# Two output banks taken in turn, and the free one lent to ScalarE, in an attention kernel planned by its own scheduler

## The chip, the cores and the metric

The kernel runs on one core of a Trainium2 chip. Its time is the device time of one execution in microseconds (us), as the median of several runs. Five engines work side by side, each through its own list of instructions in order: TensorE (PE, matmuls; PEld is its weight load), VectorE (DVE), ScalarE (ACT), GpSimd (POOL) and SyncE (SP, which here issues the transfers). They wait for each other by semaphores. Matmuls write to PSUM, which has eight banks of 512 fp32 columns on each of 128 partitions.

## The reference

Attention with normalised queries and keys over 32 heads, 2048 positions and 20 elements a head, bfloat16 in and out:

```python
B, H, S, D = 1, 32, 2048, 640        # Dh = D // H = 20
qn = q / (jnp.sqrt((q * q).sum(axis=-1, keepdims=True)) + eps)
kn = k / (jnp.sqrt((k * k).sum(axis=-1, keepdims=True)) + eps)
logits = jnp.einsum('bhqd,bhkd->bhqk', qn, kn) * t[None, :, None, None]
attn = _softmax(logits, axis=-1)
return jnp.einsum('bhqk,bhkd->bhqd', attn, v)
```

The logits lie between -t and t, so no maximum is subtracted: the kernel sums exp(logit) times v, with a column of ones beside v for the denominator, and divides at the end.

## The kernel before

**Tiling.** The scores of a head are 2048 keys by 2048 queries. They are held as S^T: 128 keys on the partitions by 512 queries in one PSUM bank is a *unit*, of which a head has 64. A product with 20 elements uses 32 of TensorE's 128 rows, so up to four units' QK matmuls (row groups g) run at the same time. Four units, one of each g, make a group; the PV product of a group is four matmuls side by side in the four column groups of TensorE, which add into the four 32-partition strips of one bank, psO (`pv_mm`, L1089). All PV products of a head add into psO; then DVE transposes the bank into SBUF (`tr`, L1107), two small DVE operations divide, and SP stores.

**Two ways to the exponential.** The 16 groups of a head are shared out by DVE_TILES (L715): so many groups (5 to 8) of the head are *DVE tiles*, the rest belongs to ScalarE (*A units*, four to a group).
- A units: TensorE writes a *wave* of units into psA (five banks), and one ScalarE instruction (L1165) turns the whole wave into bfloat16 in `p_ring`, a ring of 40 slots, one unit each. Waves have 2 and 3 units by turns (WAVES, L694): even waves use banks 0 and 1 of psA (slot 0), odd waves banks 2 to 4 (slot 1). A wave's QK (`q3A`, L1073) waits for the exponential of the wave before the last, which read the same banks. Every group of four units becomes one PV group (`pvA`).
- DVE tiles: two matmuls (`q2D`, L1078) write psD (two banks). DVE reads them with an operation that makes the bit pattern of the exponential (`t1`, L1216, into `xt`), and three more phases of the same pattern are made from `xt` by integer additions: by POOL (L1246, `ss`), or by DVE (L1234, `sp`, or L1236, `ss`). A tile has four PV groups, one of each phase.

psA 5 banks, psD 2 and psO 1 are all eight banks of PSUM.

**Heads.** As there is one output bank, the first PV group of a head waits for the transpose of the head before (`pv_base`, L1100). TensorE may do QK in the meantime. Loads, norms, and the rotated copies of the keys (`kR`) for the heads ahead are made by SP and DVE beside this.

**The planner.** Nothing of the order is fixed by hand. Every instruction is a `Task` with an engine, a planned duration, dependencies and a priority (a due time counted in heads). `list_schedule` (L151) plays through the execution with these durations and writes down an order for each engine; `plan_waits` puts in the semaphore waits and `emit` the instructions. The planned duration of a matmul group is PE_MM (L712), and a change between QK and PV costs TensorE 0.097 us (L581 and L413). The choices between ready tasks depend on some twenty settings (KNOBS, L103), which change every 10 us of planned time to the values packed into STAGES (L108). When TensorE has nothing to do, the plan may put in a filler (`pvnil`, L1004), a PV group with zero weights. The waves are laid out before the planning (L787) as tasks like all others.

Of the kernel before, what the change touches and what calls it, by code (L numbers as in the profile page):

```python
# [54 lines left out]
class Task:  # L55
    __slots__ = ("eng", "fn", "dur", "deps", "pri", "name", "lat", "dma", "n", "users",
                 "start", "end", "seq", "inc", "cnt", "rows", "work", "modes", "win", "trig",
                 "alt", "parts", "parent", "rem", "glue", "room", "next", "head", "wide", "slow", "sdur", "pair", "base", "two", "need")

    def __init__(self, eng, name, fn, dur, deps, pri, lat=0.0, dma=None):  # L60
        self.eng, self.name, self.fn, self.dur = eng, name, fn, dur
        self.deps = [d for d in deps if d is not None]
        self.pri, self.lat, self.dma = pri, lat, dma
        self.inc, self.cnt = False, 0
        self.rows, self.work, self.modes = 128, 512.0, None
        self.win, self.trig = 0.0, None
        self.alt, self.parts, self.parent, self.rem = None, [], None, 0
        self.glue, self.room, self.next, self.head, self.wide = [], 0.0, None, None, None


        self.slow, self.sdur, self.pair, self.base, self.two = False, 0.0, None, dur, None

        self.need = None
# [5 lines left out]
class Program:  # L79
# [27 lines left out]
        "WAITH": (0.3, 0.1, 0.6), "BLOG": (5, 3, 4, 7, 9, 99), "PTWO": (1, 0), "STAY": (1, 0), "URGE": (3, 2, 4, 6), "BOOST": (1.0, 0.0, 0.4, 4.0), "DPV": (0.0, 0.3, 0.65, 1.0)}  # L107
    STAGES = (121198495550, 386731570679, 77123854022, 617480453033, 541694991365, 26516008980, 28188130953, 628587374903, 9557073731, 415555843896, 209498320437, 646470623202, 136583393724, 671941958076, 672324246996, 792421957682, 689380213680, 803027612629, 379997812126, 638643698950, 639121345246, 531136220444, 376259042864, 376617779119, 221897598895, 374543095684, 221362179218, 787313552789, 415913386058, 208446558798, 427204335065, 465723747116, 401404110210, 428458674786, 432937268058, 619977817991, 207993392811, 516782334303, 568560126277, 529856924852, 435260979089, 428752721390, 619855720106, 632747624100, 787539313032, 787849807561, 633115376521, 774950211778, 788266765840, 736861074358, 722791283681, 515990522269, 287562967953, 747408491084, 537279315194, 325670581757, 376196432267)  # L108

    def __init__(self):  # L110
        self.tasks = []
        self.nsw = 0
        self.filler, self.fillers = None, []

# [5 lines left out]
    def schedule(self):  # L120
        self.list_schedule()
        for f in self.tasks:
            if f.parts:
                for u in f.users:
                    u.deps = [d for d in u.deps if d is not f] + f.parts
        self.tasks = list(dict.fromkeys(t for f in self.tasks for t in f.parts or [f])) + self.fillers
# [24 lines left out]
    def list_schedule(self, until=None):  # L151
        self.stage = None
        for t in self.tasks:
# [4 lines left out]
            if t.alt:  # L158
                t.eng, t.parts, t.slow, t.dur = "DVE", [], False, t.base
        for i, t in enumerate(self.tasks):  # L160
            t.seq = i
            deps = []
            for d in t.deps:
                deps += d() if callable(d) else [d]
            t.deps = list(dict.fromkeys(deps))
            t.n = len(t.deps)
            for d in t.deps:
                d.users.append(t)
# [16 lines left out]
        def hold(e, now, dur):  # L185

            return any(now < w <= now + (self.HTR if self.tasks[q].name[:2] == "tr" else self.HOLD[e]) and now + dur > w + 0.03
                       for q, w in soon[e].items())

# [18 lines left out]

        def leave(t, now):

            for u in t.users:
                lat = t.lat if t.dma else (
                    self.SEM_LAT[t.eng] if u.eng != t.eng or t.eng == "POOL" else 0.12 if t.eng == "DVE" else 0.0)
                if u.eng == "PE" and u.name[:2] == "pv":
                    lat += self.TR_SLACK if t.name[:2] == "tr" else self.PV_SLACK
                rt[u.seq] = max(rt[u.seq], t.end + lat)
# [176 lines left out]
        left = collections.Counter(t.head for t in self.tasks if t.head is not None)  # L393
# [3 lines left out]
        def fill(now):  # L397
# [10 lines left out]
            t = self.filler()  # L408
# [3 lines left out]
            if last_pe[0] != "pv":  # L412
                t.end += max(0.0, 0.097 - (now - free["PE"]))  # L413
# [8 lines left out]
        while events or ready["POOL"]:  # L422
# [13 lines left out]
            while events and events[0][0] <= now:  # L436
                _, kind, _, t = heapq.heappop(events)
                touched.add(t.eng)
                if kind == 0:
# [3 lines left out]
            for e in touched:  # L443
# [7 lines left out]
                if e in soon:  # L451
                    wide = e == "PE" and self.QHOLD and any(
                        now < w <= now + self.QHOLD and self.tasks[q].name[2] == "A" for q, w in soon["PE"].items())
# [8 lines left out]
                if e == "PE":  # L462
# [4 lines left out]
                    else:  # L467
                        x = min(ready[e], key=lambda r: (r[0] + (0.0 if r[2].name[:2] == last_pe[0] else self.SWITCH) + (self.DPV if r[2].need and r[2].need[0] == "t" else 0.0) - (
                            self.BOOST if r[2].need and at_[r[2].need[0]] + self.URGE >= r[2].need[1] else 0.0), r[1]))
# [8 lines left out]
                elif e == "DVE" and self.CONT:  # L478
# [21 lines left out]
                    elif not sh:  # L500
                        x = min(ready[e])
                    else:
# [5 lines left out]
                        continue  # L508
                    ready[e].remove(x)
# [68 lines left out]
                if e == "PE":  # L578
                    kind = "pv" if t.rows > 128 else t.name[:2]
                    if kind != last_pe[0]:  # L580
                        t.end += max(0.0, 0.097 - (now - free["PE"]))  # L581
# [10 lines left out]
                if t.name[:3] in ("exp", "t1."):  # L592
                    at_[t.name[0]] += 1
                done += 1
                heapq.heappush(events, (t.end, 1, t.seq, t))
                if e == "DVE" and t.parent is None and t.users and t.users[0].alt and t.users[0].parts == [t]:
# [26 lines left out]
        assert until is not None or done == len(self.tasks), "dependence cycle"  # L623
# [58 lines left out]
def bass_standalone__qk_norm__prompt_kernel(  # L682
# [11 lines left out]
    WAVES = (2, 3)  # L694
    GORD = (0, 2, 1, 3)
# [16 lines left out]
    PE_MM = 0.223  # L712
    MORE = 12
    DLM = 2
    DVE_TILES = [5, 6, 6, 6, 7, 6, 7, 6, 7, 6, 7, 6, 7, 6, 7, 6, 6, 7, 6, 7, 6, 7, 6, 7, 6, 7, 6, 7, 6, 6, 7, 8]  # L715
# [9 lines left out]
    with ExitStack() as es:  # L725
# [33 lines left out]
        psA = es.enter_context(nc.psum_tensor("psA", [128, sum(WAVES) * 512], F32))  # L759
        psD = es.enter_context(nc.psum_tensor("psD", [128, 1024], F32))  # L760
        psO = es.enter_context(nc.psum_tensor("psO", [128, 512], F32))
# [25 lines left out]
        waves = []  # L787
        while not waves or waves[-1][-1] < NA - 1:
            i = waves[-1][-1] + 1 if waves else 0
            waves.append(list(range(i, min(i + WAVES[len(waves) % 2], NA))))  # L790
        wave_of = {u: w for w, us in enumerate(waves) for u in us}
# [207 lines left out]
        for i in range(NWARM):  # L999
            warm.append(add("PE", "warm", lambda e, tk: e.matmul(psO[:, :], ones[:, 0:128], ones[:, :], start=True, stop=True), PE_MM,  # L1000
# [3 lines left out]
        def null_mm(eng):  # L1004
            last = None
            for g in range(NG):
                last = eng.matmul(psO[32 * g:32 * g + 32, :], nil[:, :], ones[:, :], start=False, stop=False,  # L1007
                                  skip_group_check=True, tile_position=(0, 32 * g))
            return last
        prog.filler = lambda: Task("PE", "pvnil", lambda e, tk: null_mm(e), PE_MM, [z_nil, z_one], 0.0)  # L1010

        def first_head(rinv):
# [25 lines left out]
            tq = add("PE", "tq0", lambda e, tk: (tmm(e, psD[:, 512:1024], qsrc, 0, 2), tmm(e, psA[:, 1536:2048], qsrc, 2, 4))[1], 0.35, [nq, z_id], -200)  # L1038
            tk1 = add("PE", "tk0", lambda e, tk: tmm(e, psA[:, 2048:2560], kx[:, 0:512], 0, 2), 0.15, [nk1, z_id], -201)
            tk_ = add("PE", "tk0", lambda e, tk: tmm(e, psD[:, 0:512], kx[:, 0:512], 2, 4), 0.2, [nk, z_id], -199)  # L1040
            for i in range(NWARM2):
                warm.append(add("PE", "warm", lambda e, tk: e.matmul(psO[:, :], ones[:, 0:128], ones[:, :], start=True, stop=True), PE_MM, [tk_], -198))
            ka = add("ACT", "cpka", lambda e, tk: e.activation(
                qkT[0][:, 512:768], psA[:, 2048:2304], ACT.Copy), 0.33, [tk1], -90.5)
            q0.append(add("ACT", "cpq0", lambda e, tk: e.activation(qkT[0][:, 0:256], psD[:, 512:768], ACT.Copy), 0.33, [tq], -90))
            q0.append(add("DVE", "cpq0", lambda e, tk: e.tensor_copy(qkT[0][:, 256:512], psA[:, 1792:2048]), 0.34, [tq], -26.5))
# [42 lines left out]
        def pv_mm(eng, h, w_of, rhs_of):  # L1089
# [3 lines left out]
            for g in range(NG):  # L1093
                last = eng.matmul(psO[32 * g:32 * g + 32, :], w_of(g), rhs_of(g), start=start,  # L1094
# [5 lines left out]
        def pv_base(h):  # L1100
            return [ld_v[h]] + z_v[h % NV] + ([lambda: [trO[h - 1]]] if h else warm)

        def add_fin(h):
# [4 lines left out]
                oT_all[:, so, :, :].rearrange("p r d -> p (r d)"), psO[:, :]), 0.63,  # L1108
# [33 lines left out]
        def add_wave(w):  # L1142
            us = waves[w]
            slot = w % 2
            hs = sorted({A_units[i][0] for i in us})
            def f_qk(eng):
                last = None
                for i in range(len(us)):
                    h, r, g = A_units[us[i]]
                    last = qk_mm(eng, h, r, g, psA[:, (slot * WAVES[0] + i) * 512:(slot * WAVES[0] + i + 1) * 512])  # L1150
                return last
            deps = [act.get(w - 2)]
            for h in hs:
                deps += qk_deps([A_units[u] for u in us if A_units[u][0] == h])
            qk = add("PE", f"q3A{w}", lambda e, tk: f_qk(e), PE_MM + 0.01, deps, w - 10000.0)
            qk.rows, qk.work = 32, 128.0 * len(us)
            qks = [qk]
            for h in hs:
                qk_users[h] += qks
            p0 = us[0] % NP  # L1160
            n = len(us) * 512
            war = [pv_of_group[(u - NP) // 4] for u in us if u >= NP]
            if any(NLATE <= u < NP for u in us):
                war += norm[0] + head0 + [u for u in rot[0]] + kx_users
            act[w] = add("ACT", f"exp{w}", lambda e, tk: e.activation(  # L1165
# [184 lines left out]
```

## Time and profile before

| | us |
|---|---|
| time, median of 3 runs (lowest, highest) | 577.27 (576.94, 577.41) |
| time of the profiled execution | 577.27 |
| its span, from the first to the last instruction | 575.5 |
| first exponential of a wave starts | 8.0 |
| last exponential of a wave ends | 565.0 |
| transpose of the output, first and last start | 32.4 and 572.0 |
| POOL's idle time before its additions | 114.5 |

The granted clock of TensorE was 0.999 of full speed in the mean. The span is what the profile shows; the rest of the time of the execution, 1.8 us, lies around it. Rows of a group give the line, engine, operation, output and inputs, the shape and the count, then busy time, the mean of one in ns, and the engine's idle time just before them with what ended it. Neighbouring instructions of ScalarE overlap in the profile (a group's mean is longer than its share of the busy time), so the pace is read from start to start.

### The profile page before, as it was taken

The numbers are of one execution on the slowest core, as the hardware profiler recorded it, in microseconds if no ns is written. First come the engines' busy times: TensorE is split into PE (matmuls) and PEld (weight loads), VectorE is DVE, ScalarE is ACT, GpSimd is POOL, SyncE is SP. The second block draws the span as 40 slices with busy tenths as digits, with TensorE's granted clock in tenths as the row PEclk, the third lists the DMA queues.
The fourth block names the chain that finished last, engine by engine and source line by source line (L and its number), as shares of the span: only waits on it lengthen the run. The fifth ranks groups of instructions, "written<-read, shape, count | busy, mean of one in ns | idle before, by whom it ended". The sixth has DMA issues, their size and how long they took to land.

```text
span 575.5 us, 14801 instructions
## 1 busy us (share of the span) xinstructions
PE 554.6 (96%) x6255; PEld 160.7 (28%) x6255; DVE 556.9 (97%) x661; ACT 558.6 (97%) x497; POOL 453.0 (79%) x406
## 2 busy tenths in 40 slices
PE   7999999999999999999999999999999999999997
PEld 2222232222222222222222232222222222223333
DVE  8999999999999999999999999999999999999997
ACT  6999999999999999999999999999999999999992
POOL 6586985898598985997768795887949888688972
PEclk9999999999999999999999999999999999999999
DMA  5544513553354403653046420563205540241000
GB/s 67 65 75 84 61 16 70 88 90 31 67 85 52 76 1 72 88 64 57 2 95 75 76 35 11 100 79 69 22 21 101 72 75 2 50 80 40 2 2 18
DMA packets 190770, 32.18 MB, mean 56 GB/s; under 512 B 170608, under 2 KB 190704, under 8 KB 190704
## 3 DMA queue, kind: packets, MB, share of 16 engines
q1 hardware_dynamic: 190560, 31.15, 35.3%
q8 instruction: 49, 0.80, 0.6%
q14 instruction: 17, 0.14, 0.1%
q10 hardware_dynamic: 144, 0.08, 0.1%
HBM read 7.87 MB, written 2.62 MB: 18 GB/s over the span
## 4 chain that ended last, share of the span: by engine, by line
ACT 86%; PE 10%; POOL 1%; DVE 1%; issue 0%; POOLq 0%
ACT p_ring L1165 86%; PE psO L1094 7%; PE psA L1073 2%; PE psD L1078 1%; DVE oT L1107 0%; POOL p_ring L1053 0%; DVE ss L1236 0%; POOL pcol L829 0%; POOL vph L770 0%; DVE xt L1216 0%; POOL vaug L770 0%; DVE rs_sum L926 0%; POOL pcol L823 0%; PE psO L1007 0%; DVE o_stage L1124 0%
## 5 line engine op out<-in xcount | busy, mean ns | idle before, releaser
L1165 ACT ACTIVATE p_ring<-psA 128x1024 bf16<-128x1024 f32 x490 | 555.1, 1369 | 2.5 <-PE psA L1073 2.2
L1246 POOL INT64_ADD ss<-xt x356 | 443.8, 1265 | 114.5 <-PE psO L1094 40.9
L1216 DVE TENSOR_SCALAR xt<-psD 128x1024 int32<-128x1024 f32 x206 | 250.4, 1216 | 5.5 <-PE psD L1078 4.7
L1234 DVE TENSOR_SCALAR sp<-xt 128x1040 int32<-128x1040 int32 x155 | 188.7, 1225 | 0.5 <-PE psO L1094 0.3
L1073 PE MATMUL psA<-qkT,kR 32*128 32x512 bf16 x968 | 164.5, 384 | 8.9 <-ACT p_ring L1165 7.3
L1094 PE MATMUL psO<-ss,vph 128*32 128x512 bf16 (+1 forms) x1852 | 166.2, 393 | 0.8 <-DVE oT L1107 0.7
L1094 PE MATMUL psO<-p_ring,vaug 128*32 128x512 bf16 x1224 | 112.1, 383 | 0.4 <-DVE oT L1107 0.4
L1073 PEld LDWEIGHTS psA<-qkT,kR 32*128 32x128 bf16 x968 | 40.0, 91 | 154.3 <-ACT p_ring L1165 146.8
L1094 PE MATMUL psO<-xt,vaug 128*32 128x512 bf16 (+1 forms) x824 | 82.2, 394 | 0.6 <-DVE oT L1107 0.3
L1094 PE MATMUL psO<-sp,vph 128*32 128x512 bf16 (+1 forms) x620 | 65.1, 408 | 0.0
L1094 PEld LDWEIGHTS psO<-ss,vph 128*32 128x32 f16 x1852 | 43.8, 94 | 58.9 <-issue 34.0
L1078 PE MATMUL psD<-qP,kR 64*128 64x512 bf16 x284 | 55.4, 387 | 1.7 <-DVE xt L1216 1.5
L1073 PE MATMUL psA<-qkT 32*128 32x512 bf16 x256 | 53.6, 384 | 1.7 <-ACT p_ring L1165 1.3
L1094 PEld LDWEIGHTS psO<-p_ring,vaug 128*32 128x32 bf16 x1224 | 29.8, 94 | 40.0 <-issue 29.4
L1094 PEld LDWEIGHTS psO<-xt,vaug 128*32 128x32 bf16 x824 | 21.7, 94 | 28.8 <-issue 18.6
L1107 DVE STREAM_TRANSPOSE oT<-psO 128x512 f32<-128x512 f32 x32 | 22.9, 715 | 6.9 <-PE psO L1094 6.4
L1078 PE MATMUL psD<-qP,qkT 64*128 64x512 bf16 x128 | 24.9, 386 | 0.8 <-DVE qP L979 0.6
L1078 PEld LDWEIGHTS psD<-qP,kR 64*128 64x128 bf16 x284 | 13.6, 92 | 39.2 <-issue 22.8
L1073 PEld LDWEIGHTS psA<-qkT 32*128 32x128 bf16 x256 | 12.9, 90 | 40.8 <-ACT p_ring L1165 38.4
L926 DVE TENSOR_REDUCE rs_sum<-sq 128x64 f32<-128x1280 bf16 (+1 forms) x17 | 23.1, 1357 | 0.0
L969 DVE TENSOR_TENSOR qkn<-qk_sb,rs_r 128x1280 bf16<-128x1280 bf16 (+1 forms) x17 | 22.9, 1367 | 0.0
L1094 PEld LDWEIGHTS psO<-sp,vph 128*32 128x32 f16 x620 | 16.3, 94 | 21.2 <-issue 10.4
(66 smaller groups left out, 129.1 us busy)
## 6 DMA issues: line engine op xcount, KB each, us to landing
kR<-qkT SPq DMA_DIRECT2D x62, 96.0 KB, 2.2
kR<-qkT SPq DMA_DIRECT2D x62, 64.0 KB, 2.1
qk_sb<-in_k_dram SPq DMA_DIRECT2D x32, 80.0 KB, 3.1
vaug<-in_v_dram SPq DMA_DIRECT2D x32, 80.0 KB, 3.3
qk_sb<-in_q_dram SPq DMA_DIRECT2D x124, 20.0 KB, 2.5
out_dram<-o_stage SPq DMA_DIRECT2D x31, 80.0 KB, 1.8
kR<-qkT SPq DMA_DIRECT2D x62, 32.0 KB, 1.9
qkT<-qkn SPq DMA_TRANSPOSE x31, 3.2
```

The source lines that it names most:

```text
L926: sums.append(dv("sum", lambda e, tk, i=i, m2=m2, src=src: e.tensor_reduce(rs["sum"][:, 2 * R * i:2 * R * i + m2], src, AXIS_X, ALU.add), ...
L969: norm[h] = [dv("norm", lambda e, tk, x=x, b=b, i=i, m=m: e.tensor_tensor(qkn_all[:, b:b + m, :, :].rearrange("p n r w -> p (n r) w")[:, : ...
L1073: return eng.matmul(dst, k_of(h, c, (rho - g) % 4, ps), qkT[h % NT][ps, 0:512], tile_position=(32 * g, 0))
L1078: return eng.matmul(dst, k_of(h, c, dl, ps), qP[h % NT][ps, :], tile_position=(64 * b, 0))
L1094: last = eng.matmul(psO[32 * g:32 * g + 32, :], w_of(g), rhs_of(g), start=start, stop=False, skip_group_check=True, tile_position=(0, 32 * g))
L1107: trO[h] = add("DVE", f"tr{h}", lambda e, tk: e.transpose(oT_all[:, so, :, :].rearrange("p r d -> p (r d)"), psO[:, :]), 0.63, [lambda: pv ...
L1165: act[w] = add("ACT", f"exp{w}", lambda e, tk: e.activation(p_ring[:, p0 * 512:p0 * 512 + n], psA[:, slot * WAVES[0] * 512:slot * WAVES[0] ...
L1216: return add("DVE", name, lambda e, tk: e.tensor_scalar(dst[:, o + 2 * w0:o + 2 * (w0 + n)].bitcast(I32), psD[:, w0:w0 + n], W_MUL, add_, ...
L1234: return e.tensor_scalar(sp[:, oe, :, :].bitcast(I32)[:, :, 0:PAD], xt[0][:, bx:bx + TILE].bitcast(I32), float(PHASE_W[i]), None, ALU.add)
L1246: f.alt = lambda c, n, i=i, dst=dst: lambda e, tk: e.int64_add(dst[:, be + 2 * c:be + 2 * (c + n)].bitcast(I64), xt[0][:, bx + 2 * c:bx + ...
```

## The change

Four things change.

1. **Output banks.** psA shrinks to the two banks of slot 0. A new tensor psF has four banks: its first and its last are the output banks, of the even and of the odd heads; the two in the middle are always slot 1's. The bank that no head is adding to is lent to slot 1, whose wave then has three neighbouring banks.
2. **Waves made while planning.** A wave is no longer laid out beforehand. When the planner has an exponential end, `wave` makes the next QK and exponential for that slot (`spawn`): two units for slot 0; for slot 1 three, if the other bank is lent and its transpose will be over in time (TRW), else two. The bank is given to the next head once at most THR PV groups of the present head are unplanned, or once the ring needs the next head's PV. A wave that would pass the end of the ring is cut to what fits, or one slot is left empty. The first PV of a head then waits for the last exponential that read its bank (`tr_bank`), and no longer for the transpose of the head before.
3. **Planned durations.** PE_MM goes from 0.223 to 0.226 and the change of kind from 0.097 to 0.102.
4. **Settings.** Three knobs are new (THR, LASTB, TRW), STAGES has new values for 58 stages in place of 57, PV tasks may have several urgencies, and DVE_TILES differs for heads 8, 9, 10, 21, 22, 23 and 31: its sum is 203 in place of 206, so there are 1236 A units in place of 1224.

```diff
-    PE_MM = 0.223
+    PE_MM = 0.226
-    DVE_TILES = [5, 6, 6, 6, 7, 6, 7, 6, 7, 6, 7, 6, 7, 6, 7, 6, 6, 7, 6, 7, 6, 7, 6, 7, 6, 7, 6, 7, 6, 6, 7, 8]
+    DVE_TILES = [5, 6, 6, 6, 7, 6, 7, 6, 6, 7, 6, 6, 7, 6, 7, 6, 6, 7, 6, 7, 6, 6, 7, 6, 6, 7, 6, 7, 6, 6, 7, 7]
...
-        psA = es.enter_context(nc.psum_tensor("psA", [128, sum(WAVES) * 512], F32))
+        psA = es.enter_context(nc.psum_tensor("psA", [128, WAVES[0] * 512], F32))
+        psF = es.enter_context(nc.psum_tensor("psF", [128, 4 * 512], F32))
         psD = es.enter_context(nc.psum_tensor("psD", [128, 1024], F32))
-        psO = es.enter_context(nc.psum_tensor("psO", [128, 512], F32))
+        psO = [psF[:, 0:512], psF[:, 3 * 512:4 * 512]]
...
-                last = eng.matmul(psO[32 * g:32 * g + 32, :], w_of(g), rhs_of(g), start=start,
+                last = eng.matmul(psO[h % 2][32 * g:32 * g + 32, :], w_of(g), rhs_of(g), start=start,
...
-            return [ld_v[h]] + z_v[h % NV] + ([lambda: [trO[h - 1]]] if h else warm)
+            return [ld_v[h]] + z_v[h % NV] + ([bank_of[h]] if h else warm)
...
+        def wave(slot, old, now):
+            if state["next"] >= NA:
+                return
+            n, b, deps = 2, slot, [old] if old else []
+            if slot:
+                while state["cur"] < min(H - 1, state["given"]) and trO[state["cur"]].left:
+                    state["cur"] += 1
+                c = state["cur"]
+                f = (c + 1) % 2
+                if state["given"] <= c:
+                    at = state["at"]
+                    if c < H - 1 and (prog.pvs[c] <= prog.THR or any(
+                            A_units[unit_at[x - NP]][0] > c for x in range(at, at + 4) if x - NP in unit_at)):
+                        state["given"] = prog.given = c + 1
+                        done_with(bank_of[c + 1], lastF.get(f) or trO[c - 1], now)
+                    elif not c or trO[c - 1].end + 0.3 <= now + prog.TRW:
+                        n, b = 3, 1 if f else 0
+                        deps += [trO[c - 1]] if c else []
+            at = state["at"]
+            if at % NP + n > NP:
+                if at % NP == NP - 1:
+                    at += 1
+                else:
+                    n = NP - at % NP
+            us = list(range(state["next"], min(state["next"] + n, NA)))
...
+            src = psF[:, b * 512:(b + len(us)) * 512] if slot else psA[:, 0:len(us) * 512]
...
+            prog.spawn(qk, deps, now)
+            prog.spawn(x, [qk] + war, now)
```

## The prediction

> **What bounds the kernel now.** I read the page first: three engines are equally full, so the busy shares alone decide nothing.
>
> ```profile
> span 575.5 us, 14801 instructions
> PE 554.6 (96%) x6255; PEld 160.7 (28%) x6255; DVE 556.9 (97%) x661; ACT 558.6 (97%) x497; POOL 453.0 (79%) x406
> ACT  6999999999999999999999999999999999999992
> ACT 86%; PE 10%; POOL 1%; DVE 1%; issue 0%; POOLq 0%
> L1165 ACT ACTIVATE p_ring<-psA 128x1024 bf16<-128x1024 f32 x490 | 555.1, 1369 | 2.5 <-PE psA L1073 2.2
> L1246 POOL INT64_ADD ss<-xt x356 | 443.8, 1265 | 114.5 <-PE psO L1094 40.9
> L1216 DVE TENSOR_SCALAR xt<-psD 128x1024 int32<-128x1024 f32 x206 | 250.4, 1216 | 5.5 <-PE psD L1078 4.7
> L1234 DVE TENSOR_SCALAR sp<-xt 128x1040 int32<-128x1040 int32 x155 | 188.7, 1225 | 0.5 <-PE psO L1094 0.3
> ```
>
> The reader should see that ScalarE has work in every slice but the first and the last, and that the last (14.4 us wide) is only 2 tenths full.
>
> Second, ScalarE's groups by shape, and the start times of its 490 exponentials in the timeline:
>
> ```profile
> L1165 ACT ACTIVATE p_ring<-psA 128x1536 bf16<-128x1536 f32 x244 | 385.7, 1581 | 1.8 <-PE psA L1073 1.6
> L1165 ACT ACTIVATE p_ring<-psA 128x1024 bf16<-128x1024 f32 x246 | 284.8, 1159 | 0.6 <-PE psA L1073 0.6
> 117.35 1.57 ACT L1165 ACTIVATE p_ring<-psA 128x1536 bf16<-128x1536 f32 x1
> 118.68 1.16 ACT L1165 ACTIVATE p_ring<-psA 128x1024 bf16<-128x1024 f32 x1
> 119.59 2.52 ACT L1165 ACTIVATE p_ring<-psA 128x1536 bf16<-128x1536 f32 x2
> ```
>
> Durations overlap, so starts must be compared: 117.35 to 118.68 is a wave of three units (1.330), 118.68 to 119.59 a wave of two (0.904, to three digits the shortest and commonest step of each kind). A unit of 512 columns is thus 0.426 us and a wave's fixed part 0.904 - 2x0.426 = 0.052 us. The exponentials run from 8.00 to 564.99 us, 557.0 us; at the undisturbed steps it would be 547.2. The 9.8 us between are small: the 244 steps after a two-unit wave average 0.936 (0.032 over, 7.85 us in sum, of which 0.73 at 10.3 and 1.25 at 99.5 are single stalls), the others 0.008 over (2.0 us). A two-unit wave is barely long enough for TensorE to refill the bank group read before it. In the 80 steps close to a transpose of the output the excess is 0.65 us in all: ScalarE does not suffer from the head switch.
>
> Third, the end of the chain, two stretches of the tail, and who waits for the transposes:
>
> ```profile
> 539.14 22.68 ACT p_ring L1165 x20
> ...
> 563.63 8.32 PE psO L1094 x141
> ...
> 571.97 0.73 DVE oT L1107
> 565.00:572.00 7.00, 6.93 (x124) 4.26 (x116) 6.14 (x9) 0.00 (x0) 2.91 (x4) 1.00 0.01 2
> 572.00:575.50 3.50, 0.00 (x0) 0.00 (x0) 1.43 (x3) 0.00 (x0) 0.00 (x0) 0.83 0.23 70
> PEld psO L1094: 7.1, 20
> ```
>
> (Columns of the two stretches: length, then busy us of PE, weight loads, DVE, ACT, POOL.) ScalarE is done at 565.0, 10.5 us ahead of the end; DVE, POOL and TensorE still finish the last head. So before is bound by ScalarE's pace to 562, and then has a tail from the other path.
>
> **The change, part by part.** The profiled execution took 577.27 us, span 575.5, so 1.8 lies around the span; it is also the median of the runs, and I add 1.8 to a span.
>
> Fewer DVE tiles. DVE_TILES sums to 206 before and 203 after, so ScalarE's units go from 1224 to 1236: 12 x 0.426 = +5.1 us on ScalarE. DVE loses 3 x 1.216 (L1216) and 3 x 155/206 x 1.225 (L1234) = 6.4 us, POOL 3 x 356/206 x 1.265 = 6.6 us; both come off the path that makes the tail, none off ScalarE's.
>
> Waves. Before, 490 waves alternate 2 and 3 units. After, an odd wave has three banks only while the other output bank is lent; from the moment the bank is given to the next head until the old head's transpose has been planned, it has two. The bank is given when 2 (23 of the 58 stages), 4 (31) or 6 (4) PV groups remain. A head lasts 17.6 us (last PV of head 0 at 31.38, of head 30 at 560.66) and has some 36 PV groups, so 0.49 us each; odd waves are 2.27 us apart. From the giving, on average one to two groups, 0.5 us to the transpose and 0.72 us for it: 1.2 to 2.2 us, less the 0.2 to 0.5 by which a wave may be planned ahead. That is 1.5 to 1.8 narrow waves a switch, 51 in 31 switches, and I add 6 for waves cut at the end of the 40-slot ring, which the 2/3 pattern no longer fits. 57 units lost from odd waves give (1236+57)/2.5 = 517 waves, +27: 27 x 0.052 = +1.4 us. Bounds: one narrow wave a switch (507 waves, +0.9) and three (534, +2.3).
>
> Cover. After a two-unit wave the next one starts 0.032 late on average. Of 517 waves some 314 have two units and 203 three: 314x0.032 + 203x0.008 = 11.7 us against 9.8: +1.9. This is the least known term. From below, TensorE freed at the switches (next part) could make refills punctual: half of all excess gone is 11.7/2 - 9.8 = -4.0. From above, a TensorE that is fuller could double the 0.032: +12. I take +1.9, since the row measures just this step, and -1.0 for half of the two single stalls, which a new plan need not meet.
>
> TensorE. A wave's QK costs a change of kind both ways: PV to QK 0.328, QK to PV 0.318, less PV to PV 0.225 = 0.42 us (20th percentiles of the steps between starts). 27 x 0.42 = +11.3; three tiles less are 3 x (4 x 0.225 + 0.42) = -4.0; three PV groups more +0.7: +8.0. Against it, from the last PV of one head to the first of the next TensorE needs 46 us in 31 switches where the QKs between would need 34.5: 12 us are waiting for a transpose (27 waits of weight load or matmul name oT, 8.5 us), and a second bank lets them go. Net -4, within the 33 us of TensorE's steps above those 20th percentiles. So I charge TensorE nothing; what covers it is that slack, and without the 12 it is +8 (a rival). The first PV of a head now waits for the last exponential that read its bank, at most one wave (1.33 us); behind it in TensorE's queue stand the QKs of the next waves, and ScalarE waits for those. A three-unit QK in turn waits for the transpose that frees the lent bank. Both waits are among the bounds of the cover term.
>
> Nothing on SP's or POOL's queues or in the DMAs is moved. The first head's transposes go to other banks in the same number. The 0.226 and 0.102 in place of 0.223 and 0.097 change only the planned order; the traced PV step (0.225 to 0.229) says that they are nearer the chip, and what this is worth is in the cover's lower bound.
>
> End. ScalarE ends at 564.99 + 5.1 + 1.4 + 1.9 - 1.0 = 572.4. After its last exponential the least is: weight load 0.23, two PV groups 0.46, and, as in the trace, 4.0 from the last PV's start (571.50) to the end: 4.7. The other bound is today's 10.5. DVE's part is 6.4 us less and ScalarE ends 7.4 later, so nothing but PV is left over: near the lower end, one more PV group, 4.9. Span 577.3, time **579.1 us** (+0.3%).
>
> That ScalarE's 6.5 us (5.1 + 1.4) do not come on top whole rests on the row of stretches above: 10.5 us without a ScalarE instruction. The Trainium skill, "Perfetto Trace Analysis", Identifying the Most-Contended Engine, has occupancy name the engine to relieve first, and here it is ScalarE (97%) that gets the tiles. By that rule the sum would be rival (e), by the row it is the one above.
>
> **Rivals.** (a) Faster: TensorE, free at the switches and planned with nearer durations, is punctual, and half the excess goes. ScalarE needs 8.0 + 547.2 + 5.1 + 1.4 + 5.9 = 567.6, plus 4.9 and 1.8: 574.3. For it: 10.5 us of tail that can be shortened, 12 us of waits for the transposes. Against: ScalarE's excess is not at the switches.
> (b) No change: the terms cancel within 1 us, for instance the cover at 0 instead of +1.9: 577.2.
> (c) TensorE becomes the bound: its +8.0 is not paid back because the bank is given so late (4 groups before the end) that the wait only moves to the exponential. TensorE's last PV group, done at 571.97 now, ends at 580.0, then 3.5 and 1.8: 585.3. It decides as soon as less than 8 of the 12 us are regained while PV is late at the end. For it: TensorE has 160 PV matmuls to do after 562. Against: three tiles fewer shorten just that tail.
> (d) The lending does little: three narrow waves a switch, 534 waves, another 17 x 0.052 and 42 x 0.024 on ScalarE (+1.9): 581.0.
> (e) ScalarE sets the pace and the tail stays as long as it is: 577.27 + 5.1 + 1.4 = 583.8. For it: its share of 97% and the steps that leave no gap. Against: with three tiles less on DVE, which is busy for 6.14 of the 7.00 us after ScalarE's end, nothing keeps the tail at 10.5.
>
> **How the numbers follow.** Forecast 0.42, (a) 0.30, (b) 0.13, (c) 0.07, (d) 0.05, (e) 0.03. The forecast's own range is 577.5 to 581. The range that holds 8 of 10 runs from 573.5, just below (a), to 584.5, short of (c). Less than 0.2% (1.15 us) from 577.27 is about what a measurement cannot tell from no change. Faster takes (a): 0.30; same takes (b) and 0.02 of the forecast: 0.15; slower takes the rest, 0.55.
>
> **What would show it.** Exponentials of 1536 columns near 200 and of 1024 near 315; the last one ending near 572 and the tail 5 us long; the transposes overlapped by PV of the next head and the waits on oT gone; the steps after two-unit waves 0.03 over 0.904. Wrong would be: over 535 or under 505 waves; ScalarE's steps clearly tighter (then (a)) or with gaps behind TensorE (then (c)); a tail of still 10 us.

## The result and the profile after

The changed kernel takes 579.65 us (median of 5, 579.47 to 580.02) where the kernel before takes 577.17 in the same comparison: a ratio of 1.0043, 95% interval [1.0028, 1.0057], 2.5 us slower. The profiled execution took 580.02 us with a span of 578.3, so again 1.8 us lie around the span.

From the page of the kernel after, the same rows as before (in the numbered lines, L1269 is the exponential, L1154 PV, L1133 the A units' QK):

```profile
span 578.3 us, 14723 instructions
PE 565.1 (98%) x6193; PEld 158.8 (27%) x6193; DVE 555.5 (96%) x655; ACT 564.6 (98%) x527; POOL 449.8 (78%) x426
ACT  6999999999999999999999999999999999999994
```

ScalarE has gained 6 us of busy time and 30 instructions, and the last slice is now four tenths full in place of two: it works longer into the end. ScalarE's groups by shape:

```profile
L1269 ACT ACTIVATE p_ring<-psF 128x1536 bf16<-128x1536 f32 x196 | 322.5, 1645 | 1.6 <-PE psF L1133 1.6
L1269 ACT ACTIVATE p_ring<-psA 128x1024 bf16<-128x1024 f32 x260 | 318.7, 1226 | 0.7 <-PE psA L1133 0.7
L1269 ACT ACTIVATE p_ring<-psF 128x1024 bf16<-128x1024 f32 x64 | 79.0, 1234 | 0.0
```

The third row is new: 64 odd waves had to do with two banks. There are 196 + 260 + 64 = 520 waves. The chain's end, and then who waited for the transposes (L1167; us in total, times):

```profile
568.49 1.03 PE psF L1154 x16
569.84 4.87 PE psF L1154 x77
574.73 0.73 DVE oT L1167
...
575.77 0.49 DVE o_stage L1184
```

```profile
PEld psF L1133: 0.7, 2
PEld psD L1138: 0.5, 2
```

No PV row waits for a transpose any more (8.5 us in 27 waits before); what is left are four QK waits, 1.2 us. The last exponential ends at 571.06 and the span 7.23 us later. Set against before, from the start times of the exponentials:

| us | before | after | difference |
|---|---|---|---|
| first exponential starts | 8.00 | 8.32 | +0.32 |
| units (0.426 each) | 1224 | 1236 | +5.11 |
| waves (0.052 each) | 490 | 520 | +1.56 |
| excess over these bare steps | 9.84 | 8.94 | -0.90 |
| last exponential ends | 564.99 | 571.06 | +6.07 |
| PV groups that start after it | 29 | 15 | |
| from there to the end (the tail) | 10.55 | 7.23 | -3.32 |
| span | 575.54 | 578.29 | +2.75 |

So the change costs ScalarE 6.7 us, spares it 0.9 us of waiting, and the tail gives back 3.3. The excess is what the steps from start to start take beyond 0.426 us a unit and 0.052 us a wave, summed up.

### The profile page after: what moved, and what is told of

Read it like the earlier page. It is cut to its first block, busy times and chain, and to the rows that moved or that the text cites. A ratio compares the mean times of both kernels' runs of the same rounds, so it can differ in the third digit from the quotient of the medians.

```text
span 578.3 us, 14723 instructions
## 1 busy us (share of the span) xinstructions
PE 565.1 (98%) x6193; PEld 158.8 (27%) x6193; DVE 555.5 (96%) x655; ACT 564.6 (98%) x527; POOL 449.8 (78%) x426
## 4 chain that ended last, share of the span: by engine, by line
ACT 86%; PE 11%; DVE 2%; issue 0%
ACT p_ring L1269 86%; PE psF L1154 6%; PE psF L1133 1%; PE psA L1133 1%; PE psD L1138 1%; PE psF L1060 1%; DVE ss L1360 1%; DVE xt L1340 0%; DVE oT L1167 0%; DVE rs_sum L986 0%; DVE vph L946 0%; DVE qP L1039 0%; DVE ones L835 0%; DVE o_stage L1184 0%; PE psF L1094 0%
## 5 line engine op out<-in xcount | busy, mean ns | idle before, releaser
L1269 ACT ACTIVATE p_ring<-psF 128x1536 bf16<-128x1536 f32 (+1 forms) x260 | 401.5, 1544 | 1.6 <-PE psF L1133 1.6
L1269 ACT ACTIVATE p_ring<-psA 128x1024 bf16<-128x1024 f32 x260 | 318.7, 1226 | 0.7 <-PE psA L1133 0.7
L1154 PE MATMUL psF<-ss,vph 128*32 128x512 bf16 (+1 forms) x1784 | 160.6, 394 | 0.0
L1154 PE MATMUL psF<-p_ring,vaug 128*32 128x512 bf16 x1236 | 110.5, 383 | 0.0
L1133 PE MATMUL psF<-qkT,kR 32*128 32x512 bf16 x567 | 88.8, 384 | 3.3 <-ACT p_ring L1269 1.2
L1133 PE MATMUL psA<-qkT,kR 32*128 32x512 bf16 x413 | 85.4, 384 | 1.8 <-ACT p_ring L1269 0.3
L1154 PE MATMUL psF<-xt,vaug 128*32 128x512 f16 (+1 forms) x812 | 82.1, 395 | 0.0
L1154 PE MATMUL psF<-sp,vph 128*32 128x512 bf16 (+1 forms) x652 | 68.0, 407 | 0.0
L1154 PEld LDWEIGHTS psF<-ss,vph 128*32 128x32 f16 x1784 | 40.5, 94 | 58.5 <-issue 43.7
L1133 PEld LDWEIGHTS psF<-qkT,kR 32*128 32x128 bf16 x567 | 21.8, 90 | 87.9 <-ACT p_ring L1269 85.7
L1133 PEld LDWEIGHTS psA<-qkT,kR 32*128 32x128 bf16 x413 | 20.6, 91 | 77.1 <-ACT p_ring L1269 75.8
L1154 PEld LDWEIGHTS psF<-p_ring,vaug 128*32 128x32 bf16 x1236 | 29.1, 94 | 41.9 <-issue 33.1
L1167 DVE STREAM_TRANSPOSE oT<-psF 128x512 f32<-128x512 f32 x32 | 22.7, 709 | 8.9 <-PE psF L1154 8.8
L1133 PE MATMUL psF<-qkT 32*128 32x512 bf16 x149 | 30.1, 384 | 1.1 <-ACT p_ring L1269 0.5
L1154 PEld LDWEIGHTS psF<-xt,vaug 128*32 128x32 bf16 x812 | 21.3, 94 | 28.0 <-issue 24.0
L1133 PE MATMUL psA<-qkT 32*128 32x512 bf16 x107 | 25.9, 384 | 0.4 <-ACT p_ring L1269 0.2
```

Of the source, the lines that this page charges most:

```text
L1133: return eng.matmul(dst, k_of(h, c, (rho - g) % 4, ps), qkT[h % NT][ps, 0:512], tile_position=(32 * g, 0))
L1154: last = eng.matmul(psO[h % 2][32 * g:32 * g + 32, :], w_of(g), rhs_of(g), start=start, stop=False, skip_group_check=True, tile_position=( ...
L1167: trO[h] = add("DVE", f"tr{h}", lambda e, tk: e.transpose(oT_all[:, so, :, :].rearrange("p r d -> p (r d)"), psO[h % 2]), 0.63, [lambda: p ...
L1269: x = Task("ACT", f"exp{w}", lambda e, tk: e.activation(p_ring[:, p0 * 512:p0 * 512 + m], src, ACT.Exp, scale=LN2), EXP0 + m / 1200.0, [], w)
```

## The experiments

The theory was that ScalarE's added work is what the change costs, while TensorE and DVE matter only for the excess and the tail. The rival was that TensorE, with 30 more waves of QK and full in the chain from 529 us on, sets the time after. The planner makes it hard to undo one part: a different duration or tile count gives another order for everything behind it. So most experiments hold the planned order and make one engine's instructions shorter, longer or more.

### TensorE lighter: PV matmuls of half width

```diff
-                last = eng.matmul(psO[32 * g:32 * g + 32, :], w_of(g), rhs_of(g), start=start,
+                x, n = rhs_of(g), 512 if start else 256
+                x = x[:, 0:n] if len(x.shape) == 2 else x[:, 0:n // PAD]
+                last = eng.matmul(psO[32 * g:32 * g + 32, 0:n], w_of(g), x, start=start,
```

Before:

> Before, its order of instructions held, but every PV matmul except the first of a head covers only 256 of its 512 columns (the other half of the queries is left out of the sum). TensorE is lighter by about 1100 groups x 0.11 = 120 us. Theory (ScalarE sets the pace to its last exponential, TensorE and DVE only the tail): ScalarE's excess of 9.8 us over its bare steps falls to 2 to 6, its last exponential ends at 558 to 562, DVE's work after it keeps the span at 568 to 574. Rival (TensorE sets the pace): the span falls by far more than 10 us, below 560.

After:

> After, with the same halved PV matmuls. Theory: the last exponential ends at 566 to 570 (ScalarE's 12 units and 30 waves more than before stay, 6 to 7 us), the tail shrinks from 7.2 to 4 to 5, span 571 to 574. Rival (TensorE's added QK set the time of after): last exponential no more than 2 us behind that of before with halved PV, span below it.

Measured: spans of 598.1 and 607.5 us, 23 and 29 us longer than the kernels they were made from; a second execution of each took longer still (622.8 and 631.1 us at a mean clock of 0.788 and 0.773). Neither theory had this. The row of the granted clock says why; from the page of before with half-width PV, and the same row of after with it:

```profile
PEclk9669999999758995799999999999999999955557
```

```profile
PEclk9555555599999999999999999999999995555999
```

TensorE's clock falls to about half for long stretches (0.884 and 0.865 in the mean, 0.999 in both kernels as they are). Two stretches of before with half-width PV (length, then busy us of PE, weight loads, DVE, ACT, POOL, then the clock):

```profile
460.00:520.00 60.00, 49.11 (x671) 16.56 (x667) 59.08 (x68) 60.00 (x55) 49.28 (x37) 1.00 0.31 54
532.00:575.00 43.00, 43.00 (x389) 12.46 (x386) 34.77 (x33) 35.82 (x30) 29.91 (x28) 0.50 0.03 8
```

At full clock TensorE is busy 49 of 60 us; once the clock is at 0.50 it is busy all the time and drags ScalarE and DVE down. The Trainium skill, "TensorE: Matmul & The Clock Gate", Part 1: The HAM clock gate, lets the clock fall after at least one idle window of about 3.4 us. Here the largest gap between two matmuls was 0.96 us, and the clock fell all the same, so an idle window of that length is not needed. As a test of the theories by their times these two runs are void: they changed the clock as well as the work. The trace says a little more. ScalarE's excess is 33 us in before with half-width PV, but the 366 steps well inside the stretches at full clock hold only 4.1 us of it; the same steps of before as it is hold 6.9. In after, 345 such steps hold 4.2 us, against 4.4. So nearly all of the loss lies in the stretches at half clock, and at full clock a lighter TensorE takes little off ScalarE's steps.

### ScalarE lighter: exponentials of three quarters

```diff
+            cut = n // 4 if us[0] >= 60 else 0
...
-                p_ring[:, p0 * 512:p0 * 512 + n], psA[:, slot * WAVES[0] * 512:slot * WAVES[0] * 512 + n], ACT.Exp, scale=LN2),
+                p_ring[:, p0 * 512:p0 * 512 + n - cut], psA[:, slot * WAVES[0] * 512:slot * WAVES[0] * 512 + n - cut], ACT.Exp, scale=LN2),
```

Before:

> Before, its order held, but from unit 60 on each exponential covers only the first three quarters of its wave's columns (the last quarter of each wave keeps old values). ScalarE is lighter by about 464 x 0.27 = 124 us. Theory: TensorE and DVE have 30 and 14 us of slack, so the span falls by only 5 to 20 us, to 555 to 570: all three engines are near their limits. Rival (ScalarE alone binds): it falls by over 40 us.

After, with the same edit in `wave`:

> After, with the same shortened exponentials. Theory: TensorE, which is full from 529 us on and makes the 7.2 us tail, stops the fall soon: 3 to 15 us, to 563 to 575. Rival (TensorE alone sets the time of after): less than 2 us.

Measured: 570.63 us (569.79 and 571.46) and 570.38 us (569.88 and 570.89), at a clock of 1.00. The engines' shares of the chain that ended last, before first, then after:

```profile
PE 47%; DVE 42%; ACT 3%; SPq 3%; issue 2%; DMA 1%; POOL 1%; DVEq 0%
```

```profile
PE 63%; DVE 31%; ACT 3%; issue 1%; POOL 1%; DVEq 0%; POOLq 0%
```

With ScalarE out of the way (81% and 83% busy) the two kernels are equal to within what two executions can tell. Before falls by 6.6 us, after by 9.3. So, in these two orders, the path through TensorE and DVE is no longer after the change than before it, 30 waves of QK more notwithstanding; the rival, which has after stand on TensorE, would have had it fall by less than 2 us. Before's fall also shows how little is to be had: 124 us less on ScalarE are worth 6.6.

### More on ScalarE in before

122 of the three-unit exponentials are issued as two instructions; nothing is left out.

```diff
-            act[w] = add("ACT", f"exp{w}", lambda e, tk: e.activation(
-                p_ring[:, p0 * 512:p0 * 512 + n], psA[:, slot * WAVES[0] * 512:slot * WAVES[0] * 512 + n], ACT.Exp, scale=LN2),
+            cuts = [0, 1024, n] if w % 4 == 1 and n == 1536 else [0, n]
+
+            def f_exp(e):
+                for a, b in zip(cuts, cuts[1:]):
+                    last = e.activation(p_ring[:, p0 * 512 + a:p0 * 512 + b], psA[:, slot * WAVES[0] * 512 + a:slot * WAVES[0] * 512 + b], ACT.Exp, scale=LN2)
+                return last
+            act[w] = add("ACT", f"exp{w}", lambda e, tk: f_exp(e),
```

> Before, order held, nothing left out: 122 of its 244 three-unit exponentials are done as two instructions (two units, then one). ScalarE gets 122 x 0.052 = 6.3 us more and nothing else changes; after's own addition to ScalarE is 6.7 (12 units, 30 waves). Theory (ScalarE's work is what the change costs): the last exponential ends 5 to 7 us later, at 570 to 572; the tail of 10.5 us takes up part, and the time goes up by 2 to 6 us, at least as much as with the change (+2.5). Rival (after is slower for another reason, TensorE's QK or its new waits): the tail takes it all, the time goes up by less than 1 us.

Measured: 583.77 us, ratio 1.0111 [1.0095, 1.0128], +6.5 us. Its ScalarE groups and the end of its chain:

```profile
L1169 ACT ACTIVATE p_ring<-psA 128x1024 bf16<-128x1024 f32 x368 | 414.5, 1226 | 1.6 <-PE psA L1073 1.6
L1169 ACT ACTIVATE p_ring<-psA 128x1536 bf16<-128x1536 f32 x122 | 201.6, 1652 | 0.6 <-PE psA L1073 0.5
L1169 ACT ACTIVATE p_ring<-psA 128x512 bf16<-128x512 f32 x122 | 96.6, 792 | 0.0
```

```profile
570.00 8.32 PE psO L1094 x141
...
578.35 0.73 DVE oT L1107
```

The price of an instruction is confirmed (6.3 us expected, the last exponential moves from 564.99 to 571.36, +6.4). The tail isn't what I expected: I had it take up a part, and it took nothing. The last run of PV is the same 8.32 us and 141 matmuls as before, 6.4 us later, and from the last exponential to the end it is 10.55 us in both. So here the tail is a property of the planned order. The likely reason is that each engine goes through its list in order and each list waits for the others, so that a delay of ScalarE shifts all that comes after.

### Less on ScalarE in after

```diff
+            cut = 16 if us[0] >= 60 else 0
...
-                p_ring[:, p0 * 512:p0 * 512 + m], src, ACT.Exp, scale=LN2), EXP0 + m / 1200.0, [], w)
+                p_ring[:, p0 * 512:p0 * 512 + m - cut], src[:, 0:m - cut], ACT.Exp, scale=LN2), EXP0 + m / 1200.0, [], w)
```

> After, order held, but from unit 60 on every exponential leaves out the last 16 columns of its wave (they keep old values): about 495 x 16/1200 = 6.6 us less on ScalarE, so that it has as much work as in before. Theory: the time falls by 3 to 6 us, to 573.5 to 576.5, below before by 0.5 to 4: two output banks and three DVE tiles less are a gain once ScalarE doesn't pay for them. Rival (TensorE sets the time of after): it falls by less than 1.5 us.

Measured: 574.16 us, ratio to before 0.9945 [0.993, 0.9959]; 5.5 us less than after, 3.1 less than before. From its ScalarE groups and its chain:

```profile
L1270 ACT ACTIVATE p_ring<-psF 128x1520 bf16<-128x1520 f32 x186 | 297.3, 1598 | 0.9 <-PE psF L1133 0.7
L1270 ACT ACTIVATE p_ring<-psA 128x1008 bf16<-128x1008 f32 x247 | 291.0, 1178 | 0.0
```

```profile
563.81 4.87 PE psF L1154 x78
568.70 0.73 DVE oT L1167
```

The last exponential ends at 564.89, where it ends in before (564.99); the tail is 7.37, as in after. With ScalarE's work brought back to what it was, the rest of the change is worth its shorter tail, 3 us. This and the run above settle the main question: ScalarE's 6.7 us pass into the time almost whole.

### More QK on TensorE in before

```diff
-                for i in range(len(us)):
+                for i in [*range(len(us))] * (2 if w % 16 == 9 else 1):
```

> Before, order held, nothing left out: the QK matmuls of 31 waves (every 16th) are issued twice in a row into the same banks with the same values, 31 x 0.23 to 0.32 = 7 to 10 us more on TensorE, like the 30 waves that after adds there. Theory: TensorE's slack takes most of it, +0 to +3 us; each doubled wave makes one exponential late by what exceeds its cover. Rival (TensorE's added QK cost the time): +5 to +10 us.

Measured: 580.87 us, ratio 1.0060 [1.0045, 1.0075], +3.6 us, somewhat over the theory's range and under the rival's. ScalarE's excess goes from 9.84 to 13.07 us, nearly all of it after two-unit waves (0.046 over the bare step in place of 0.032). A second QK takes TensorE 0.226 us from start to start, 7.0 us for the 31 waves; they cost 0.12 us each, about half, and they do so through ScalarE: the refill no longer fits under a two-unit wave. The 30 waves that the change adds bring changes of kind as well (0.42 us a wave by the prediction's steps), so this run loads TensorE less than they do. In after the excess is nonetheless no larger than in before. Whether the transposes that PV no longer waits for, the three tiles less or the new order pay for these QKs, no run here separates.

### One tile of the last head

```diff
-    DVE_TILES = [5, 6, 6, 6, 7, 6, 7, 6, 7, 6, 7, 6, 7, 6, 7, 6, 6, 7, 6, 7, 6, 7, 6, 7, 6, 7, 6, 7, 6, 6, 7, 8]
+    DVE_TILES = [5, 6, 6, 6, 7, 6, 7, 6, 7, 6, 7, 6, 7, 6, 7, 6, 6, 7, 6, 7, 6, 7, 6, 7, 6, 7, 6, 7, 6, 6, 7, 7]
```

> Before with one DVE tile less, the last head's (8 to 7), which is the one tile that can be moved without changing the plan ahead of it: ScalarE gets 4 units (1.7 us) and 2 waves (0.1), DVE and POOL lose 2.2 us each, TensorE 1.1. Theory: ScalarE's end moves from 565 to 566.8, the tail falls from 10.5 to 8.5, the time stays within 1 us or falls by up to 1. Rival (tail set by ScalarE's last exponential): +1.8.

Measured: 577.74 us, ratio 1.0007 [0.9998, 1.0017]: the same to within the measurement. ScalarE's end moves to 567.02 (+2.03, of which 0.10 is a later first wave), the tail falls to 8.86 (-1.69) with 22 PV groups behind the last exponential in place of 29. The gain and the loss of a tile nearly cancel. The change takes the same tile from the last head, so about half of its shorter tail (1.7 of 3.3 us) is to be had from this tile alone.

### The two halves of the change, planned anew

Each half alone needs a plan of its own, so STAGES was searched again for each, by trying single values in the planner and keeping what shortens its planned end. Before with after's tiles:

> Before with one output bank and its own planned durations, but with after's DVE_TILES (203 tiles), STAGES searched anew for it. ScalarE has 1236 units in 495 waves (+5.1 and +0.3 us); the plan leaves 5 PV groups behind the last exponential in place of 29. Theory (time = ScalarE's end + 3.8 + 0.23 for each PV group left): end at 569.5 to 573, tail 5, time 577 to 580. Rival (three tiles less are a gain, the waves the loss): below 576.

After with before's tiles:

> After with before's DVE_TILES (206 tiles, 1224 units), STAGES searched anew for it: two output banks, lending and traced durations alone, 516 waves. The plan leaves 22 PV groups behind the last exponential. Theory: ScalarE has 5.1 us less than after, but the tail is 22 x 0.23 + 3.8 = 8.9: time 578.5 to 582. Rival (the tiles are the loss): 576 or less.

After with nothing changed but STAGES:

> After with all else equal and only STAGES searched further: 519 waves, 12 PV groups behind the last exponential in place of 15. Theory: -0.7 for the tail and up to -0.3 besides, 578.4 to 579.3, still slower than before. Rival (the settings, not the structure, make after slow): 577 or less.

| | waves | excess us | last exponential ends | PV groups left | tail us | span us | time us, ratio to before |
|---|---|---|---|---|---|---|---|
| before, 203 tiles | 495 | 13.4 | 573.80 | 4 | 4.77 | 578.57 | 579.02, 1.0033 [1.0023, 1.0044] |
| after, 206 tiles | 516 | 12.2 | 568.66 | 22 | 8.83 | 577.49 | 579.09, 1.0032 [1.0020, 1.0044] |
| after, searched on | 519 | 8.7 | 570.54 | 10 | 6.19 | 576.73 | 578.52, 1.0022 [1.0013, 1.0032] |

The profiled execution of the first took 580.3 us, the second longest of its eight; the others are near their medians. In its trace the granted clock is 0.50 from 306.0 to 309.4 us, and ScalarE's excess between 305 and 310 us is 1.5 us, where before has none. The executions of this kernel at a mean clock of 0.997 took 580.3 and 580.5 us, the six at 1.0 took 578.5 to 579.3. All three times lie in the theory's ranges; ScalarE's end in the first is 0.8 us beyond its range, no more than this drop of the clock accounts for. The PV groups left are 4 and 10 in the first and third, where the plans had 5 and 12. The end of the chain shows the tails, before with 203 tiles first, then after with 206:

```profile
572.60 2.40 PE psO L1094 x37
575.02 0.73 DVE oT L1107
```

```profile
567.16 6.73 PE psF L1154 x109
573.92 0.73 DVE oT L1167
```

Three tiles moved to ScalarE push its end out and leave hardly any PV behind it; two output banks with the old tiles leave ScalarE's end earlier and a long run of PV. Each half alone is about 1.9 us slower than before. How much of that is the half and how much a plan that was searched less than the one of before, these runs don't tell: the excess, 13.4 (11.9 without the drop of the clock) and 12.2 us, is larger than in either kernel.

### The same work in another order

```diff
-    PE_MM = 0.223
+    PE_MM = 0.2235
```

> Before with one planned duration changed by 0.2% (PE_MM 0.223 to 0.2235) and STAGES left as they are: the same work, another order. Theory (STAGES fit one plan and no other): 10 to 20 us slower, more than all that the change itself moves. Rival (the order hardly matters): within 2 us.

Measured: 593.45 us, ratio 1.0280 [1.0259, 1.0300], +16.3 us. ScalarE's 490 waves are the same; their excess is 25 us in place of 9.8, with single steps up to 3.0 us late. Not everything else is the same: the plan put in 20 more fillers (148 filler matmuls in place of 68) and shared the additions between DVE and POOL in another way. The clock was at 0.50 for 3.4 us from 87.8 us on, but from 84 to 110 us the excess is 4.3 us against 1.4 in before, so most of it lies elsewhere. Settings that were searched for one plan are worth this much, six times the change under study. None of the kernels that compute everything was faster than before.

## Why the prediction was right, and where it was not

The forecast was 579.1 us, slower by 0.3%; measured were 579.65 and 0.43%. Point by point:

- **Units**: +5.1 forecast, 12 more units found; the tile count fixes it.
- **Waves**: 517 forecast, 520 found, +1.4 against +1.56; the 57 units I had taken from odd waves are 64, one for each odd wave of two banks. What an instruction costs ScalarE was confirmed by splitting 122 of them.
- **Cover**: +1.9 forecast with -1.0 for single stalls, and -0.9 found for both together. I gave every step after a two-unit wave the 0.032 of the steps in before; the 196 that lead to three units show 0.029, but the 127 that lead to two units only 0.015. The single stalls are still there (1.05 at 10.6 us and 1.09 at 100.9). So ScalarE ended at 571.06, not 572.4.
- **TensorE**: charged nothing, and with ScalarE lighter the two kernels end together. Its busy time rose by 10.5 us (554.6 to 565.1). The waits for the transposes went, as forecast. But the doubled QK showed that its slack is not free: about half of the added QK time comes out at ScalarE.
- **End**: 4.9 forecast, 7.23 found. This is the term that was mis-sized, and its reason was wrong too. I wrote that ScalarE ends 7.4 us later and DVE has 6.4 us less to do, so that "nothing but PV is left over". That much came true (from 570 to 575 us DVE is busy for 0.27 us, the start of the transpose), but it doesn't say how much PV. DVE's busy time fell by 1.4 us and not 6.4, POOL's by 3.2 and not 6.6. And where only ScalarE got more work, its lateness didn't shorten the tail at all: the 10.5 us without a ScalarE instruction, on which the forecast rested that ScalarE's 6.5 us would not come on top whole, are not slack, and 6.3 us more on ScalarE cost 6.5. What differs is the planned order. In the six plans of this list the tail is 3.8 us plus 0.23 for each PV group that starts after the last exponential: 29, 22, 22, 15, 10 and 4 groups give 10.5, 8.9, 8.9, 7.25, 6.1 and 4.7, measured were 10.55, 8.86, 8.83, 7.23, 6.19 and 4.77. This rule stood on record before the three plans of the table above were run. After has 15 groups left, where I had taken three.

The two errors, 1.3 us too long and 2.3 too short, partly cancelled: a span of 577.3 forecast, 578.3 found. That the time came out within 0.6 us is in this part luck; the terms for ScalarE's units and waves were right by their reasons. Of the rivals, (e) had the right price for ScalarE and, as the split exponentials show, the right mechanism where the order is held, but not the shorter tail of the new plan; (b) is out, as the interval of the ratio lies above 1; (c) is out by the time itself and by the runs with shortened exponentials; (d) had 534 waves, and there are 520; and (a) would have needed half the excess to go; a tenth went.

Left open: whether two output banks alone, planned as carefully as the kernel before, would gain or lose, and which part of the change shortens the tail.

## What to carry to other kernels

Where one engine goes from its first to its last instruction nearly without a gap, and all lists are in a fixed order, work added to that engine can pass into the time whole, even if it stands idle at the end: the end is the order's, and moves along. Here 6.3 us more on ScalarE cost 6.5. Work taken away need not come back: 124 us less gained 6.6. So count what the bound engine gets, then count what the order leaves behind its last instruction. In six plans here the PV groups left gave the tail to 0.1 us; ScalarE's own end needs the excess as well (8.7 to 13.4 us), which no count gave. And before a part of a planned kernel is undone, see what the planner makes of any small change; holding the order and changing one engine's instructions tells causes apart more cheaply, as long as the clock stays what it was.

## What was not expected of the hardware

Halving the width of PV made the kernel 23 us slower (span 598.1 against 575.5), since TensorE's granted clock fell to 0.50 for tens of microseconds although no gap between its matmuls was longer than 0.96 us. In these runs a lighter TensorE went with a lower clock (0.884 and 0.865 in the mean, against 0.999); what in its load decides this, they don't show. Two plans with all the work lost the clock as well, for 3.4 us each (before with 203 tiles from 306.0 us, before with the other planned duration from 87.8 us), and no gap between their matmuls in the 10 us ahead was longer than 0.8 us.
